# An attention and gated-MLP kernel on one Trainium2 core: the exponentials' output in natural token order instead of chunk order

## The chip, the core and the metric

The kernel runs on one core of a Trainium2 chip. The metric is the device time of one execution, in microseconds (us). Engines are named as in the profile: PE (TensorE matmul), PEld (its weight loads), DVE (VectorE), ACT (ScalarE), POOL (GpSimd), SP (SyncE, which here only issues transfers).

## The reference

For 8 batches, 12 heads, 448 tokens and a head width of 64:

```
q_n, k_n = rmsnorm(q, g_q), rmsnorm(k, g_k)
attn     = softmax(q_n @ k_n.T / 8)
x        = (attn @ v), heads side by side          # [8, 448, 768]
h        = relu(x @ w_in);  u, v = halves of h     # [8, 448, 512] each
v_n      = (v - mean(v)) / sqrt(var(v) + 1e-6)
v_s      = w_spatial @ v_n + b_spatial             # mixes the 448 tokens
out      = (u * v_s) @ w_out                       # [8, 448, 768] float32
```

## The kernel before

Work comes in 24 groups of four heads (three groups to a batch). A load (`op_L`) puts the queries or the keys of a group into a tile `raw` of 128 partitions: 64 partitions for each of two heads, times two heads in the free dimension (`r`). Partition p holds the seven token rows 7p to 7p+6 of its head one after the other, so token t is at (p, c) with t = 7p + c. The c are called chunks here: a chunk is 64 tokens, each seven apart from the next.

For a group the steps are: squares and their sums (`op_Q`, `op_R`), the inverse root (`op_I`, `op_J`), the multiplication `nrm<-raw,rs` (`op_N`), a transposition through SP's queue into `qT` and `kr` (`op_T`, line 493), and a copy of the keys with the gains (`op_Z`). After the transposition the tokens lie along the free dimension in chunk order: first the 64 tokens of chunk 0, then those of chunk 1, and so on (position 64c + p).

`op_S` (line 518) computes the scores of one key chunk for the four heads into two PSUM banks, the 64 keys of two heads along the partitions and the 448 queries along the free dimension. `op_E` (line 526) is one ACT instruction that takes the exponential of both banks, 128 partitions by 896 elements, and writes them in bfloat16 to a tile `et`. There are 7 of these for each group, 168 in all. The sums and the products with v (`op_s`, `op_a`, `op_b`, line 551) run over `et` with the queries as the moving dimension; `op_D` and `op_d` make the reciprocal of the sum (a logarithm and an exponential on ACT), and `op_X` (line 580) multiplies it in and writes `xt`, whose columns are the tokens.

From `xt` on, a batch is one set of matrix products: `op_V` and `op_W` (lines 596 and 625) give v for tiles of 128 tokens, `op_c`, `op_B`, `op_M`, `op_m`, `op_A` normalise it, `op_U` (line 662) gives u, `op_H` (line 676) multiplies with the spatial weights, `op_G` gates, `op_O` (line 690) multiplies with `w_out`, `op_o` evicts to a tile `os` of 128 rows by 768, and `op_t` (lines 711 and 714) stores it.

Since nothing reorders the tokens on the way, all of that is in chunk order as well. An output tile m holds chunk 2m in partitions 0 to 63 and chunk 2m+1 in partitions 64 to 127; in the result, the rows of a chunk are seven apart. So `op_t` stores a full tile with two transfers of 64 rows each, and the last tile (64 rows, chunk 6) with one or two more. The spatial weights have to be in chunk order too. They are loaded in the setup as `w_sp` (line 337; its space is the tile `gt` in the profile's names), transposed by PE in `op_Y` (line 360), whose weight operand picks columns seven apart, and copied to `w_spT` by `op_y` as they come; the bias is read with a step of seven elements and written densely by `op_wx` (both through the helper at lines 373 and 375).

The order of the instructions is written out: `PLAN` is one list of words, such as `E.0.1/0/a` (operation E, group 0, chunk unit 1, slot 0, engine ACT), and every engine's queue takes its own operations in that order. PSUM banks and tile slots are given in the words. The scores of a unit come a few words ahead of its exponential, in banks that an earlier exponential has read. `t` words, squares, reciprocals, evictions and exponentials are interleaved in it; SP issues loads, transpositions and stores in one queue. `port` puts waits between DVE and POOL instructions that use tiles in SBUF, in the order of the list.

Of the kernel before, what the change touches and what calls it, by code (L numbers as in the profile page):

```python
# [11 lines left out]
AF = mybir.ActivationFunctionType  # L12
# [150 lines left out]
def kernel(  # L163
# [14 lines left out]
    B, H, S, D = q.shape  # L178
# [3 lines left out]
    C = 7  # L182
    T = 64
    TAIL = 384
    scale = 1.0 / math.sqrt(D)
    pe, act, dve, pool, sync = nc.tensor, nc.scalar, nc.vector, nc.gpsimd, nc.sync
    engines = {"a": act, "v": dve, "g": pool, "s": sync}
# [4 lines left out]
    ps = psp.tile([128, 8, 512], FP, name="ps")  # L192

    def several(name, n, shape, dt):
        return [const.tile(shape, dt, name=f"{name}{i}") for i in range(n)]
# [7 lines left out]
    ets = several("et", SLOTS["et"], [128, 2, S], BF)  # L203
# [15 lines left out]
    oss = several("os", SLOTS["os"], [128, DM], FP)  # L219
# [7 lines left out]
    w_sp = gt_all.rearrange("p n f s -> p (n f) s")[0:64, 0:C]  # L227
    w_spT = const.tile([128, 4, S], BF, name="w_spT")
# [117 lines left out]

    def op_wx(sl, e):
        assert where["wb"]
        copy(engines[e], w_spT[64:65, 3, :].rearrange("q (c p) -> q c p", p=T),
             oss[-1][64:65, 0:S].rearrange("q (p c) -> q c p", c=C))  # L350
        where["wx"] = True

    def op_Y(sl, e, m):

        n = 1 if m == 3 else 2
        where["Y", m] = sl[0]
        p_ = ps[:, sl[0], :].bitcast(BF)
        for a in range(n):
            for c in range(C):
                pe.matmul(out=p_[64 * a:64 * a + 64, T * c:T * c + T],  # L360
                          lhsT=w_sp[:, c, :].rearrange("q (p c) -> q c p", c=C)[:, 2 * m + a, :],
                          rhs=ident[0:64, 0:64], is_transpose=True, start=(c == 0), stop=(c == C - 1),
                          tile_position=(0, 64 * a))

    def op_y(sl, e, m):
        n = 1 if m == 3 else 2
        p_ = ps[:, where.pop(("Y", m)), :].bitcast(BF)[0:64 * n, 0:S]
        copy(engines[e], w_spT[0:64 * n, m, :], p_)
        where["wT", m] = True

    def copy(eng, out, in_):
        if eng is act:
            act.activation(out=out, in_=in_, func=AF.Copy, bias=0.0, scale=1.0)  # L373
        else:
            eng.tensor_copy(out=out, in_=in_)  # L375
# [147 lines left out]
    def op_E(sl, e, G, u):  # L523
        a, b = where.pop(("S", G, u))
        where["et", G, u] = sl[0]
        act.activation(out=ets[sl[0]], in_=ps[:, a:b + 1:b - a, 0:S], func=AF.Exp, bias=0.0, scale=1.0)  # L526

    def et_of(G, r, c):
        if G or c == 6:
# [69 lines left out]
    def tail_at(b, h):  # L599

        return 0 if b == B - 1 and h == 0 else 64
# [97 lines left out]
             ps[rows, where.pop(("O", b, m, h))[0], 0:384])  # L699
        where["o", b, m, h] = True  # L700

    out_c = [out[b].rearrange("(p c) m -> c p m", c=C) for b in range(B)]

    def op_t(sl, e, b, m):
        t = oss[where["os", b, m]]
        assert where["o", b, m, 0] and where["o", b, m, 1]
        if m == 3:
            for n, at in enumerate(sorted({tail_at(b, 0), tail_at(b, 1)})):
                cols = [h for h in range(2) if tail_at(b, h) == at]
                cols = slice(384 * cols[0], 384 * cols[-1] + 384)  # L710
                engines[(e or "ss")[n]].dma_start(out=out_c[b][6][:, cols], in_=t[at:at + 64, cols])
            return
        for par in range(2):
            engines[(e or "ss")[par]].dma_start(out=out_c[b][2 * m + par], in_=t[64 * par:64 * par + 64])

    def op_z(sl, e, n):
        dummies(sl[0], n)
# [5 lines left out]
    for word in PLAN.split():  # L723
        name, sl, e = (word.split("/") + ["", ""])[:3]
# [32 lines left out]
```

## Time and profile before

| | |
|---|---|
| three runs | 275.09, 276.58 and 278.78 us, median 276.58 |
| the profiled execution | 275.98 us; span from first to last instruction 274.2 us |
| busy: PE, ACT, DVE, POOL | 257.9, 217.8, 203.8, 145.0 us |
| mean granted TensorE clock | 0.985 |

Busy time is the sum of the time in which an engine had an instruction under way. Matmuls are pipelined and their ends are modelled, so PE's busy time is an upper figure. Neighbouring instructions of one engine overlap a little, so a mean duration times a count is somewhat more than the busy time of a group. "Idle before" of a group is time in which its engine stood still just ahead of it, with the instruction that ended the wait.

### The profile page before, as it was taken

To read this page: it belongs to the slowest core of one execution; us is meant where nothing else is said; L and a number is where in the kernel's file an instruction comes from. 1 tells how busy PE (TensorE), PEld (TensorE's weight loads), DVE (VectorE), ACT (ScalarE), POOL (GpSimd) and SP (SyncE) were. 2 spreads that over 40 slices of the span, in tenths; PEclk is the share of its full clock that TensorE was granted. 3 is DMA by queue.
4 is the path that set the end of the run, shared out by engine and by line. 5 is a ranking of instruction groups with operands and counts; after the bars stand their busy time and mean duration, and the time that the engine had idled before them with its cause. 6 is when DMAs were issued, how large, how long until landed. Compare 5 with 4: busy or idle time off the path is not lost.

```text
span 274.2 us, 10148 instructions
## 1 busy us (share of the span) xinstructions
PE 257.9 (94%) x4372; PEld 137.5 (50%) x4389; DVE 203.8 (74%) x355; ACT 217.8 (79%) x357; POOL 145.0 (53%) x122
## 2 busy tenths in 40 slices
PE   7788999999899999999999999989999999999992
PEld 7565564465345455344454454444454545455550
DVE  3788899879859998987985698946976284748730
ACT  4489899999889999988998999988899965330632
POOL 3092994698745898957875669649950000000000
PEclk9959999999999999999999999999999999999998
DMA  7999998999969999999799999976986400114586
GB/s 208 319 344 273 260 171 119 295 204 245 167 145 168 376 177 187 198 251 184 232 184 267 286 246 241 175 95 61 194 114 141 117 2 2 31 29 115 154 279 204
DMA packets 63072, 51.14 MB, mean 187 GB/s; under 512 B 39601, under 2 KB 58674, under 8 KB 63026
## 3 DMA queue, kind: packets, MB, share of 16 engines
q1 hardware_dynamic: 54770, 42.22, 65.4%
q0 software_dynamic: 8256, 8.27, 19.3%
q8 instruction: 34, 0.56, 0.8%
q14 instruction: 12, 0.10, 0.1%
HBM read 38.55 MB, written 11.01 MB: 181 GB/s over the span
## 4 chain that ended last, share of the span: by engine, by line
PE 42%; POOL 13%; DMA 12%; DVE 10%; ACT 10%; issue 10%; SPq 1%; ACTq 0%; POOLq 0%; DVEq 0%
PE ps L551 8%; PE ps L690 7%; POOL nrm L438 7%; PE ps L662 7%; DMA vt<-in_v_dram 6%; ACT et L526 6%; PE ps L676 6%; PE ps L596 5%; PE ps L518 5%; POOL sqt L394 5%; DMA raw<-in_q_dram 3%; DVE ss L405 3%; DMA kr<-nrm 3%; PE ps L625 3%; POOL vt L326 2%
## 5 line engine op out<-in xcount | busy, mean ns | idle before, releaser
L526 ACT ACTIVATE et<-ps 128x896 bf16<-128x896 f32 x168 | 146.1, 923 | 13.4 <-PE ps L518 11.4
L438 POOL TENSOR_TENSOR nrm<-raw,rs 128x896 bf16<-128x896 f32 x40 | 67.3, 1691 | 29.0 <-ACT rs L423 9.4
L518 PE MATMUL ps<-qT,kT 64*32 64x448 bf16 x1344 | 61.1, 357 | 3.2 <-DVE kT L476 1.1
L551 PE MATMUL ps<-et,vt 64*32 64x448 bf16 x1344 | 52.1, 350 | 2.5 <-DMA vt<-in_v_dram 1.0
L394 POOL TENSOR_TENSOR sqt<-raw 128x896 f32<-128x896 f32 x28 | 46.8, 1683 | 13.8 <-DVE vn L653 9.3
L405 DVE TENSOR_REDUCE ss<-sqt 128x14 f32<-128x896 f32 x46 | 48.5, 1076 | 2.9 <-ACT sqt L392 1.2
L662 PE MATMUL ps<-xt,w_in 128*128 128x448 bf16 x192 | 43.4, 353 | 0.2
L518 PEld LDWEIGHTS <-kT 64*32 64x32 bf16 x1344 | 22.2, 90 | 31.7 <-issue 22.5
L690 PE MATMUL ps<-w_out,gt 128*128 128x384 bf16 x192 | 36.5, 326 | 0.1
L580 DVE TENSOR_TENSOR xt<-ps,rc 128x448 bf16<-128x448 f32 x48 | 27.9, 618 | 11.5 <-ACT rc L574 6.9
L596 PE MATMUL ps<-w_in,xt 128*128 128x512 bf16 x127 | 33.9, 380 | 0.9 <-issue 0.3
L551 PEld LDWEIGHTS <-vt 64*32 64x32 bf16 x1344 | 24.9, 92 | 16.2 <-issue 4.2
L373 ACT ACTIVATE os<-ps 128x384 f32<-128x384 f32 (+1 forms) x34 | 16.3, 491 | 15.2 <-PE ps L690 14.6
L551 PE MATMUL ps<-et,ones 64*32 64x448 bf16 x672 | 27.8, 349 | 0.0
L676 PE MATMUL ps<-w_spT,vn 128*128 128x448 bf16 (+1 forms) x128 | 27.7, 353 | 0.2 <-DVE xt L580 0.2
L662 PEld LDWEIGHTS <-w_in 128*128 128x128 bf16 x192 | 17.2, 97 | 20.8 <-issue 7.4
L690 PEld LDWEIGHTS <-gt 128*128 128x128 bf16 x192 | 18.1, 98 | 15.6 <-issue 2.7
L681 DVE TENSOR_TENSOR gt<-ps,us 128x448 bf16<-128x448 f32 x32 | 19.2, 619 | 9.0 <-PE ps L676 5.9
L637 DVE BATCH_NORM_STATS2 s<-vs 128x6 f32<-128x512 bf16 (+1 forms) x32 | 21.9, 683 | 1.6 <-ACT vs L587 1.1
L375 DVE COPY os<-ps 128x384 f32<-128x384 f32 (+1 forms) x30 | 16.5, 555 | 8.9 <-PE ps L690 5.5
L326 POOL DMA_DIRECT2D vt<-in_v_dram x34 | 23.0, 681 | 0.0
L589 DVE TENSOR_SCALAR vs<-ps 128x512 bf16<-128x512 f32 (+1 forms) x24 | 16.3, 683 | 7.4 <-PE ps L596 3.5
(63 smaller groups left out, 253.5 us busy)
## 6 DMA issues: line engine op xcount, KB each, us to landing
out_dram<-os SPq DMA_DIRECT2D x55, 192.0 KB, 3.2
raw<-in_k_dram SPq DMA_DIRECT2D x23, 448.0 KB, 5.9
raw<-in_q_dram SPq DMA_DIRECT2D x23, 448.0 KB, 7.0
vt<-in_v_dram POOLq DMA_DIRECT2D x14, 224.0 KB, 7.3
vt<-in_v_dram POOLq DMA_DIRECT2D x20, 112.0 KB, 5.4
w_in<-in_moe_w_in_dram POOLq DMA_DIRECT2D x8, 192.0 KB, 12.8
w_out<-in_moe_w_out_dram POOLq DMA_DIRECT2D x1, 768.0 KB, 8.2
raw<-in_k_dram SPq DMA_DIRECT2D x2, 224.0 KB, 3.7
```

The source lines that it names most:

```text
L326: pool.dma_start(out=vts[b % 2][64 * halves[0]:64 * halves[0] + 64 * len(halves), g].rearrange("p r c d -> p r (c d)"), in_=src)
L394: port(eng, eng.tensor_tensor(out=t, in0=x, in1=x, op=ALU.mult))
L405: dve.tensor_reduce(out=sss[G % 3][:, i].rearrange("p r c -> p (r c)"), in_=sqt[where.pop(("sq", G, i))].rearrange("p r (c d) -> p (r c) d ...
L438: port(eng, eng.tensor_tensor(out=nrm[sl[0]].rearrange("p c r d -> p r c d"), in0=raw[where["raw", G, i]].rearrange("p r (c d) -> p r c d" ...
L518: pe.matmul(out=ps[at:at + 32, sl[n], 0:S], lhsT=kT[64 * r:64 * r + 64, c, 64 * hh + 32 * x:64 * hh + 32 * x + 32], rhs=qT[64 * r:64 * r + ...
L526: act.activation(out=ets[sl[0]], in_=ps[:, a:b + 1:b - a, 0:S], func=AF.Exp, bias=0.0, scale=1.0)
L551: pe.matmul(out=ps[32 * l:32 * l + 32, where[kind, G][0], 0:S], lhsT=w, rhs=et_of(G, r, c)[at:at + 64], start=(n == 1), stop=(n == C), til ...
L580: dve.tensor_tensor(out=xts[b % 2][:, 2 * g + half, :], in0=ps[:, where.pop(("ab"[half], G))[0], 0:S], in1=rcs[where["rc", G]], op=ALU.mult)
L596: pe.matmul(out=ps[:, bank, :], lhsT=xts[b % 2][:, j, 128 * m:128 * m + 128], rhs=w_in[:, j % 2, j // 2, DH:], start=(n == 1 and j == 2 * ...
L662: pe.matmul(out=ps[:, bank, 0:S], lhsT=w_in[:, j % 2, j // 2, 128 * f:128 * f + 128], rhs=xts[b % 2][:, j, :], start=(n == 1 and j == 2 * ...
L676: pe.matmul(out=ps[:, sl[0], 0:S], lhsT=vns[b % SLOTS["vn"]][rows, m, 128 * f:128 * f + 128], rhs=w_spT[rows, m, :], start=(m == 0), stop= ...
L690: pe.matmul(out=ps[:, sl[0], 0:384], lhsT=gts[b % 2][:, f, 128 * m:128 * m + 128], rhs=w_out[:, f, 384 * h:384 * h + 384], start=(f == 0), ...
```

## The change

The exponential writes its result through a permuted view. It still reads the two PSUM banks in chunk order, one element after the other, and puts the element of (c, p) at position 7p + c: two elements that follow each other in the stream land 7 bfloat16 elements apart. From there on the tokens are in natural order. An output tile m holds rows 128m to 128m+127 and is stored with one transfer; the last tile holds rows 384 to 447. The spatial weights are read densely by `op_Y` and written with a step of seven by `op_y`; the bias is copied densely. `PLAN`, slots and the order of all instructions stay as they are; of each pair of stores of a full tile one is left.

```diff
     def op_wx(sl, e):
-        copy(engines[e], w_spT[64:65, 3, :].rearrange("q (c p) -> q c p", p=T),
-             oss[-1][64:65, 0:S].rearrange("q (p c) -> q c p", c=C))
+        copy(engines[e], w_spT[64:65, 3, :], oss[-1][64:65, 0:S])
...
     def op_Y(sl, e, m):
-                          lhsT=w_sp[:, c, :].rearrange("q (p c) -> q c p", c=C)[:, 2 * m + a, :],
+                          lhsT=w_sp[:, c, 128 * m + 64 * a:128 * m + 64 * a + 64],
...
     def op_y(sl, e, m):
-        copy(engines[e], w_spT[0:64 * n, m, :], p_)
+        copy(engines[e], w_spT[0:64 * n, m, :].rearrange("q (p c) -> q c p", c=C),
+             p_.rearrange("q (c p) -> q c p", c=C))
...
     def op_E(sl, e, G, u):
-        act.activation(out=ets[sl[0]], in_=ps[:, a:b + 1:b - a, 0:S], func=AF.Exp, bias=0.0, scale=1.0)
+        act.activation(out=ets[sl[0]].rearrange("q r (p c) -> q r c p", c=C),
+                       in_=ps[:, a:b + 1:b - a, 0:S].rearrange("q r (c p) -> q r c p", c=C),
+                       func=AF.Exp, bias=0.0, scale=1.0)
...
-    out_c = [out[b].rearrange("(p c) m -> c p m", c=C) for b in range(B)]
-
     def op_t(sl, e, b, m):
...
-                engines[(e or "ss")[n]].dma_start(out=out_c[b][6][:, cols], in_=t[at:at + 64, cols])
+                engines[(e or "ss")[n]].dma_start(out=out[b][TAIL:S, cols], in_=t[at:at + 64, cols])
             return
-        for par in range(2):
-            engines[(e or "ss")[par]].dma_start(out=out_c[b][2 * m + par], in_=t[64 * par:64 * par + 64])
+        engines[(e or "s")[0]].dma_start(out=out[b][128 * m:128 * m + 128], in_=t)
```

## The prediction

> **What bounds the kernel now.** I read the page first, then busy time by stretch, then the chain of waits, then the groups of instructions by shape.
>
> ```profile
> span 274.2 us, 10148 instructions
> PE 257.9 (94%) x4372; PEld 137.5 (50%) x4389; DVE 203.8 (74%) x355; ACT 217.8 (79%) x357; POOL 145.0 (53%) x122
> ACT  4489899999889999988998999988899965330632
> ...
> PE 42%; POOL 13%; DMA 12%; DVE 10%; ACT 10%; issue 10%; SPq 1%; ACTq 0%; POOLq 0%; DVEq 0%
> ```
>
> Over the whole span PE is the busiest engine and leads the chain that ended last. ACT's 79% is an average over two stages: its row of slices stands at 8 or 9 up to slice 32 and falls off after. All exponentials start between 14.4 and 228.9 us (first row below), so I cut the span there (second and third row; columns after the stretch: its length, then busy us and instructions of PE, PEld, DVE, ACT, POOL; granted clock, DMA share, GB/s):
>
> ```profile
> L526 ACT ACTIVATE et<-ps x168: 896/917/982, 14.4 to 228.9; 128x896 bf16<-128x896 f32 x168
> ...
> 14.40:230.00 215.60, 208.83 (x3847) 107.64 (x3869) 172.00 (x287) 196.91 (x312) 141.30 (x112) 0.99 0.94 193
> 230.00:274.20 44.20, 38.76 (x354) 20.63 (x340) 23.32 (x48) 14.17 (x32) 0.00 (x0) 0.98 0.44 126
> ```
>
> In the first stretch ACT works 196.9 of 215.6 us. It has 18.7 us of slack, 9%. Time added to ACT there beyond that slack lengthens the kernel, whatever the chain shows today. In the last 44 us ACT has slack in plenty, and no exponential runs.
>
> ```profile
> L526 ACT ACTIVATE et<-ps 128x896 bf16<-128x896 f32 x168 | 146.1, 923 | 13.4 <-PE ps L518 11.4 <-PE ps L551 1.1
> L373 ACT ACTIVATE os<-ps 128x384 f32<-128x384 f32 x27 | 13.1, 493 | 14.8 <-PE ps L690 14.6
> ...
> ACT et L526 <- PE ps L518: 11.4, 29, 1.1
> ```
>
> The exponentials are 146.1 of ACT's 196.9 us. ACT stood still before them for 13.4 us, of which 11.4 us are 29 waits for scores, none over 1.1 us. The two rows also give ACT's price for each element when it writes densely: (923 - 493) / (896 - 384) = 0.84 ns, on 170 ns that don't depend on the width.
>
> **The exponential's write.** The count of exponentials, their input and their width stay; only the place of each written element moves, to 14 bytes from the one before. No instruction of the trace writes single elements apart, so the price has to be bounded from both sides. A permutation as such is free where the runs are long:
>
> ```profile
> L438 DVE TENSOR_TENSOR nrm<-raw,rs 128x896 bf16<-128x896 f32 x6 | 6.4, 1088 | 1.5 <-POOL nrm L438 1.1 <-POOL nrm L446 0.4
> L394 DVE TENSOR_TENSOR sqt<-raw 128x896 f32<-128x896 f32 x5 | 5.3, 1086 | 1.3 <-POOL nrm L438 0.7 <-POOL sqt L394 0.6
> ```
>
> Line 438 writes a permuted tile in runs of 64 elements and takes 1088 ns, the dense line 394 takes 1086. So the lower end is no price at all: 923 ns as before. Single elements apart are read at two places in the setup:
>
> ```profile
> L360 PEld LDWEIGHTS <-gt 64*64 64x64 bf16 x49 | 4.2, 193 | 2.7 <-issue 1.9 <-DMA gt<-in_moe_w_spatial_dram 0.8
> L551 PEld LDWEIGHTS <-vt 64*32 64x32 bf16 x1344 | 24.9, 92 | 16.2 <-issue 4.2 <-DMA vt<-in_v_dram 1.9
> L625 PEld LDWEIGHTS <-gt 128*64 128x64 bf16 x64 | 6.0, 109 | 1.5 <-issue 0.3
> ...
> L375 DVE CAST w_spT<-os 1x448 bf16<-1x448 f32 x1 | 1.0, 971 | 0.0
> L411 DVE TENSOR_REDUCE ss<-sqt 128x7 f32<-128x448 f32 x4 | 2.4, 618 | 1.9 <-ACT sqt L392 1.9
> L405 DVE TENSOR_REDUCE ss<-sqt 128x14 f32<-128x896 f32 x46 | 48.5, 1076 | 2.9 <-ACT sqt L392 1.2 <-POOL sqt L394 1.2
> ```
>
> Line 360 loads 64 columns that are 7 bfloat16 elements apart, the very step of the new write. It takes 193 ns, where 32 dense columns take 92 and 64 dense ones 109. Dense columns add (109 - 92) / 32 = 0.53 ns each, which leaves 75 ns fixed; the stepped ones come to (193 - 75) / 64 = 1.84 ns each, or, with all of the 92 ns as fixed, 1.58. The bias copy on DVE reads 448 float32 elements 28 bytes apart in 971 ns; dense reads on that engine cost (1076 - 618) / 448 = 1.02 ns each on 161 fixed, so the stepped read costs (971 - 161) / 448 = 1.81 ns. Two engines with different dense prices arrive at 1.6 to 1.8 ns for an element that stands alone. That looks like a price of the memory access, so I expect a write to pay it too: upper end 1.84 ns, lower end of a paid price 1.58. Between "free" and "paid" I take "paid", because the nearest row, line 360, has the same step and the same type; within 1.58 to 1.84 I take 1.68, twice ACT's own 0.84 (an element on every second step, an estimate). One exponential then takes 170 + 896 x 1.68 = 1675 ns, 0.753 us more, and 168 of them add 126.4 us (111 at 1.58, 150 at 1.84).
>
> [...]
>
> **What absorbs it.** The longer exponential gives PE 0.75 us more for each next set of scores. The 29 waits average 0.39 us, so I let all 11.4 us vanish; the ends are nothing and the whole slack of 18.7. No other engine hides more: ACT then has 196.9 + 126.4 = 323.3 us of work in that stretch, PE 208.8, DVE 172.0, POOL 141.3, and what waits behind the exponentials in ACT's queue (the roots for POOL's `nrm`, the reciprocals for DVE's `xt`, evictions) comes later by as much. PE's products read `et` densely before and after, which costs nothing new.
>
> **The stores.** 24 of the 48 transfers of line 714 go.
>
> ```profile
> L714 SPq DMA_DIRECT2D out_dram<-os x48: 466/590/1426, 125.6 to 269.5; - x48
> ...
> SPq L493 <- POOL nrm L438: 68.3, 22, 14.4
> ...
> 255.63 14.45 SPq L714 DMA_DIRECT2D out_dram<-os  x20
> 270.18 1.18 SPq L711 DMA_DIRECT2D out_dram<-os  x2
> ...
> 268.14 0.49 ACT L373 ACTIVATE os<-ps 128x384 f32<-128x384 f32 x1 [0.47 <-PE ps L690]
> 268.90 0.99 ACT L373 ACTIVATE os<-ps 64x384 f32<-64x384 f32 x2 [0.28 <-PE ps L625]
> ```
>
> At 0.590 us each that frees 14.2 us of SP's queue, but SP waits far longer for others (68.3 us for `nrm` alone), so inside the span it is worth nothing; were SP never waiting, it would be at most those 14.2 us. At the end the last eviction is done at 268.90 + 0.99 = 269.89 and the last two stores start at 270.18, since the store ahead holds the queue until 270.08. One issue less lets them start at 269.89: 0.3 us gained. Against it, one transfer of 384 KB may land later than two of 192:
>
> ```profile
> out_dram<-os SPq DMA_DIRECT2D x55, 192.0 KB, 3.2
> raw<-in_k_dram SPq DMA_DIRECT2D x23, 448.0 KB, 5.9
> ```
>
> The last full tile is evicted at 268.14 + 0.49 = 268.63; with the 5.9 us of the larger loads it lands at 274.5, 0.3 us past today's end. I take -0.3, ends -0.3 and +0.3.
>
> **The setup.** The 49 weight loads of line 360 become dense, 193 to 109 ns: 4.1 us of loads; 21 of them stand on the chain with their matmuls (second row below: start and length in us), 21 x 84 ns = 1.8 us at most. The bias copy falls from 971 to about 161 + 448 x 1.02 = 618 ns. Against this the four copies to `w_spT` write single elements:
>
> ```profile
> L360 PE MATMUL ps<-ident,gt 64*64 64x64 bf16 x49 | 4.4, 274 | 1.3 <-DVE w_spT L375 0.9 <-DMA gt<-in_moe_w_spatial_dram 0.4
> 14.12 1.90 PE ps L360 x21
> ...
> L676 PE MATMUL ps<-w_spT,vn x128: 349/353/363, 63.5 to 262.5; 128*128 128x448 bf16 x96, 65*128 65x448 bf16 x32
> L375 DVE COPY w_spT<-ps x2: 381/387/393, 13.7 to 21.4; 128x448 bf16<-128x448 bf16 x2
> L373 ACT ACTIVATE w_spT<-ps x2: 524/530/536, 15.2 to 16.4; 64x448 bf16<-64x448 bf16 x1, 128x448 bf16<-128x448 bf16 x1
> ```
>
> At 1.84 ns the DVE copies take up to 161 + 824 = 985 ns each (+1.2 us in all), and ACT's two 170 + 753 = 923 (+0.8). Line 676 reads `w_spT` only from 63.5 us on; PE waited for such a copy once (0.9 us). These nearly cancel: I take 0, ends -1.8 and +2.
>
> **Sum.** 274.2 + 126.4 - 11.4 - 0.3 = 388.9 us of span. The profiled execution took 275.98, 1.8 more than its span and 0.6 below the median of the runs; with that I predict 391 us. Ends of this case: 274.2 + 111 - 18.7 - 2.1 + 1.8 = 366, and 274.2 + 150 + 2.3 + 1.8 = 428.
>
> **The rivals.**
> *The write is free* (13%). ACT's output side takes single elements at 0.84 ns, the exponential stays at 923 ns, and the stores decide: -0.3 at the end, 276 us, not slower than before; the point from which this turns is an added price under 11.4 us in all, 0.08 ns an element. For it: the trace shows stepped reads only, and ACT's write may be decoupled from its stream. Against it: line 360. The setup's and the stores' ends make 272 to 278 of it; over 2% faster needs 5.5 us of the 14.2 that SP is spared, which I give 3 of the 13%. [...]
>
> *Half the price* (12%): the write overlaps partly, halfway between the ends, 63 us: 274.2 + 63 - 11.4 + 1.8 = 328. Nothing in the trace speaks for a middle value but that reads and writes may differ.
>
> *TensorE's clock falls and PE becomes the bound as well* (12%).
>
> ```profile
> 10.00:11.00 1.00, 0.47 (x8) 0.12 (x8) 1.00 (x2) 0.00 (x0) 0.00 (x0) 1.00 1.02 293
> 11.00:12.00 1.00, 0.61 (x11) 0.52 (x8) 0.47 (x1) 0.29 (x1) 0.00 (x0) 1.00 1.05 380
> 12.00:13.00 1.00, 1.00 (x19) 0.74 (x17) 0.31 (x1) 0.97 (x3) 0.00 (x0) 1.00 1.06 384
> 13.00:14.00 1.00, 0.22 (x8) 0.17 (x1) 1.00 (x2) 0.29 (x2) 0.82 (x1) 0.59 1.06 382
> 14.00:15.00 1.00, 0.88 (x10) 0.87 (x9) 0.60 (x2) 0.94 (x3) 1.00 (x3) 0.50 1.05 376
> ...
> 19.00:20.00 1.00, 1.00 (x24) 0.23 (x24) 1.00 (x2) 0.44 (x1) 1.00 (x3) 0.50 1.19 270
> ```
>
> After 4 us at 57% busy the granted clock was 0.50 for some 6 us. Behind a slow ACT, PE is 208.8 / 330 = 63% busy. At half clock its work for one exponential doubles, 2 x 208.8 / 168 = 2.49 us against ACT's 323.3 / 168 = 1.92; if half of the exponentials fall in such times, 84 x 0.57 = 48 us are added: 439. Against it: gaps will be short and spread, and a slower PE is a busier one.
>
> *More than two steps an element* (6%): three, 2.52 ns, add 253 us and give about 517.
>
> **How the numbers follow.** The main case has 57%. Leaving out the free write (13%) and the three steps (6%), the range goes from just under half the price, 325, to just over the clock's rival, 445. Slower by over 2%, which is about what a measurement here can tell from no change (the runs spread over 1.3%), holds in all cases but the free write: 87%. Within 2%: 10%. Faster: 3%.
>
> **What would show it.** Right: the group of line 526 at about 1675 ns with the same 896 elements, ACT over 95% busy from 14 us to about 45 us before the end, its 11.4 us of waits for scores nearly gone, PE around 60% there, the last stage still some 44 us. The price is a step's if the mean is near 1675 or 2430 and not between. Wrong: line 526 near 923 ns. The clock's rival: PEclk at 0.5 to 0.8 in the middle slices. The stores: 24 issues of 384 KB, and the gap between last eviction and last store closed.

## The result: 2.59 times slower

The changed kernel takes 713.14 us (median of 6 runs, 712.32 to 713.56), the kernel before 275.83 us in the same session. The ratio is 2.588, with a 95% interval of 2.579 to 2.597. The direction was forecast, the size was not: 391 us were predicted, with 445 as the upper end. Here and below, medians are over all runs of a kernel; the ratios leave out disturbed ones, so the two can differ by a few tenths of a per cent.

The page of the changed kernel, busy time, slices of ACT and of the granted clock, and the chain that ended last:

```profile
span 710.5 us, 10114 instructions
PE 407.7 (57%) x4372; PEld 168.9 (24%) x4389; DVE 209.9 (30%) x355; ACT 660.8 (93%) x357; POOL 145.2 (20%) x122
ACT  5999999999999999999999999999999999989623
PEclk8555556655757755675676795585587575576799
...
ACT 75%; issue 13%; PE 9%; DMA 1%; DVE 1%; SPq 0%; ACTq 0%; DVEq 0%
```

The page cuts the span into 40 slices; from the 2nd to the 37th ACT is now busy for 80% or more, and after the last exponential some 45 us are left, as before. One stretch of 100 us (columns as in the prediction), the groups by shape and the waits:

```profile
100.00:200.00 100.00, 55.36 (x568) 19.71 (x565) 27.39 (x45) 99.73 (x49) 22.81 (x16) 0.62 0.28 64
...
L526 ACT ACTIVATE et<-ps 128x896 bf16<-128x896 f32 x168 | 594.4, 3838 | 5.2 <-PE ps L518 4.8
L375 DVE COPY w_spT<-ps 128x448 bf16<-128x448 bf16 x2 | 3.8, 1876 | 0.0
...
POOL nrm L438 <- ACT rs L423: 233.9, 17, 33.5
PE ps L518 <- ACT et L526: 173.8, 91, 3.2
...
ACT et L526 <- PE ps L518: 4.8, 7, 1.5
```

One exponential went from 923 to 3838 ns. The group's busy time rose from 146.1 to 594.4 us, by 448.3 us. That is the whole loss: ACT's busy time rose by 660.8 - 217.8 = 443.0 us, its idle time fell from 56.4 to 49.7, and the span rose by 436.3. (168 times 3838 ns would be 645 us: neighbouring exponentials overlap, and one takes 594.4 / 168 = 3.54 us of ACT's time.) Everyone waits for ACT now (PE for banks and `et`, POOL for the roots), and ACT waits for scores 4.8 us in all.

### The profile page after: what moved, and what is told of

It is laid out like the page before. It is cut to its first block, busy times and chain, and to the rows that moved or that the text cites. A ratio compares the mean times of both kernels' runs of the same rounds, so it can differ in the third digit from the quotient of the medians.

```text
span 710.5 us, 10114 instructions
## 1 busy us (share of the span) xinstructions
PE 407.7 (57%) x4372; PEld 168.9 (24%) x4389; DVE 209.9 (30%) x355; ACT 660.8 (93%) x357; POOL 145.2 (20%) x122
## 4 chain that ended last, share of the span: by engine, by line
ACT 75%; issue 13%; PE 9%; DMA 1%; DVE 1%; SPq 0%; ACTq 0%; DVEq 0%
ACT et L526 69%; PE ps L692 2%; PE ps L553 2%; PE ps L664 1%; ACT sqt L392 1%; DMA raw<-in_q_dram 1%; PE ps L678 1%; ACT rc L576 1%; PE ps L518 1%; ACT rc L572 1%; ACT os L373 1%; PE ps L598 1%; DVE ss L405 1%; ACT rs L423 1%; ACT w_spT L373 0%
## 5 line engine op out<-in xcount | busy, mean ns | idle before, releaser
L526 ACT ACTIVATE et<-ps 128x896 bf16<-128x896 f32 x168 | 594.4, 3838 | 5.2 <-PE ps L518 4.8
L518 PE MATMUL ps<-qT,kT 64*32 64x448 bf16 x1344 | 98.3, 485 | 204.6 <-ACT et L526 173.8
L553 PE MATMUL ps<-et,vt 64*32 64x448 bf16 x1344 | 81.1, 473 | 12.4 <-ACT et L526 8.7
L664 PE MATMUL ps<-xt,w_in 128*128 128x448 bf16 x192 | 62.9, 472 | 14.1 <-ACT et L526 11.3
L553 PE MATMUL ps<-et,ones 64*32 64x448 bf16 x672 | 50.2, 558 | 15.2 <-ACT et L526 7.8
L692 PE MATMUL ps<-w_out,gt 128*128 128x384 bf16 x192 | 47.8, 395 | 9.3 <-ACT et L526 7.3
L598 PE MATMUL ps<-w_in,xt 128*128 128x512 bf16 x127 | 46.6, 491 | 6.8 <-ACT et L526 3.4
L678 PE MATMUL ps<-w_spT,vn 128*128 128x448 bf16 (+1 forms) x128 | 41.0, 473 | 9.5 <-ACT et L526 9.3
L591 DVE TENSOR_SCALAR us<-ps 128x448 bf16<-128x448 f32 x22 | 13.5, 621 | 50.5 <-PE ps L664 50.3
L553 PEld LDWEIGHTS <-ones 64*32 64x32 bf16 x672 | 18.2, 129 | 33.4 <-issue 32.9
```

The source lines that it names most:

```text
L518: pe.matmul(out=ps[at:at + 32, sl[n], 0:S], lhsT=kT[64 * r:64 * r + 64, c, 64 * hh + 32 * x:64 * hh + 32 * x + 32], rhs=qT[64 * r:64 * r + ...
L526: act.activation(out=ets[sl[0]].rearrange("q r (p c) -> q r c p", c=C), in_=ps[:, a:b + 1:b - a, 0:S].rearrange("q r (c p) -> q r c p", c= ...
L553: pe.matmul(out=ps[32 * l:32 * l + 32, where[kind, G][0], 0:S], lhsT=w, rhs=et_of(G, r, c)[at:at + 64], start=(n == 1), stop=(n == C), til ...
L591: dve.tensor_relu(out=out, in_=in_)
L598: pe.matmul(out=ps[:, bank, :], lhsT=xts[b % 2][:, j, 128 * m:128 * m + 128], rhs=w_in[:, j % 2, j // 2, DH:], start=(n == 1 and j == 2 * ...
L664: pe.matmul(out=ps[:, bank, 0:S], lhsT=w_in[:, j % 2, j // 2, 128 * f:128 * f + 128], rhs=xts[b % 2][:, j, :], start=(n == 1 and j == 2 * ...
```

## The experiments

### Writes and reads by themselves

A kernel with five instructions of each kind, one after the other on their engine, from PSUM or from a tile in SBUF. Beside them run only stores of a constant and, at the start, fills of the input tiles by POOL. ACT's and DVE's writes were not under way together; ACT's reads, though, ran beside DVE's first writes. In short:

```
a_perm:  out = t.rearrange("q r (p c) -> q r c p"), in = two banks, as in the change
a_exp / d_copy(type, step, run): out = tile viewed as (p, step)[:, :, 0:run], in = PSUM, dense
a_read:  out dense, in = two banks read 64 elements apart
reads:   out dense bfloat16, in = tile in SBUF, one element of every 7
```

> Nothing of the reference is computed; ACT and DVE instructions stand alone, five of each kind, and write bfloat16 or float32 elements out of PSUM densely, 2, 4, 7 or 8 elements apart, and in runs of two or four with gaps between the runs; some read single elements and write densely. In the changed kernel the exponential took 3838 ns, (3838 - 170) / 896 = 4.1 ns for each element. Theory A (a price of small pieces): every written piece below some width costs about 4 ns by itself, on ACT and DVE alike; then the permuted exponential takes about 3.7 us here too, with steps of 2, 4, 7 and 8 alike, runs of two or four bfloat16 elements cost a half, a quarter or less for each element, and float32 elements 7 apart are cheap, 1.7 ns or less. Theory B (a price of hops): any hop costs 4 ns, so float32 elements 7 apart cost as much as bfloat16 ones, and small steps (2, 4) cost less than 7. Theory C (contention in the full kernel): alone, the permuted exponential takes 1.0 to 1.7 us, and the rest came from the other engines. Reads of single elements, the row of the prediction: A and B expect 1.6 to 1.9 ns an element on DVE for float32 7 apart if the bias copy told the truth, 1.0 if it had only waited for POOL. The exponential that reads PSUM 64 elements apart and writes densely: 923 ns if such reads are free, 1.7 us or more if not.

The groups by shape; `ab` and `af` are ACT's bfloat16 and float32 writes, `vb` and `vf` DVE's, `arb`, `arf`, `vrf` reads:

```profile
L48 ACT ACTIVATE ab_dense<-ps 128x896 bf16<-128x896 f32 x5 | 4.6, 917 | 1.9 <-DVE ps L32 1.8
L52 ACT ACTIVATE ab_perm<-ps 128x896 bf16<-128x896 f32 x5 | 18.2, 3631 | 0.1
L57 ACT ACTIVATE ab_readperm<-ps 128x896 bf16<-128x896 f32 x5 | 4.8, 970 | 0.1
L48 ACT ACTIVATE ab_two<-ps 128x896 bf16<-128x896 f32 x5 | 5.8, 1161 | 0.1
L48 ACT ACTIVATE ab_four<-ps 128x896 bf16<-128x896 f32 x5 | 10.7, 2147 | 0.1
L48 ACT ACTIVATE ab_seven<-ps 128x896 bf16<-128x896 f32 x5 | 18.3, 3652 | 0.1
L48 ACT ACTIVATE ab_eight<-ps 128x896 bf16<-128x896 f32 x5 | 20.9, 4182 | 0.1
L48 ACT ACTIVATE ab_run_two<-ps 128x896 bf16<-128x896 f32 x5 | 5.2, 1030 | 0.1
L48 ACT ACTIVATE af_two<-ps 128x448 f32<-128x448 f32 x5 | 2.8, 562 | 0.1
L48 ACT ACTIVATE af_seven<-ps 128x448 f32<-128x448 f32 x5 | 4.8, 962 | 0.1
L79 DVE CAST vb_seven<-ps 128x448 bf16<-128x448 f32 x5 | 9.5, 1903 | 0.1
L79 DVE COPY vf_seven<-ps 128x448 f32<-128x448 f32 x5 | 4.7, 949 | 0.1
L97 ACT ACTIVATE arb_dense<-sarb_dense 128x448 bf16<-128x448 bf16 x5 | 2.9, 574 | 0.1
L97 ACT ACTIVATE arb_seven<-sarb_seven 128x448 bf16<-128x448 bf16 x5 | 4.5, 896 | 0.1
L97 ACT ACTIVATE arf_seven<-sarf_seven 128x448 bf16<-128x448 f32 x5 | 5.0, 1009 | 0.1
L99 DVE CAST vrf_dense<-svrf_dense 128x448 bf16<-128x448 f32 x5 | 2.0, 392 | 0.1
L99 DVE CAST vrf_seven<-svrf_seven 128x448 bf16<-128x448 f32 x5 | 2.8, 565 | 0.1
```

The permuted exponential alone takes 3631 ns, so theory C falls: the 0.2 us more that the mean in the full kernel shows is within what neighbours overlap there. Less the prediction's 170 ns, the bfloat16 steps 2, 4, 7 and 8 cost 1.11, 2.21, 3.89 and 4.48 ns an element. That grows with the step, which theory A did not expect. Float32 at step 7 costs 1.77 ns on ACT, so theory B, which expected 4, falls too. A's main point stands: pairs of bfloat16, 28 bytes apart, are written in 1030 ns. DVE pays the same as ACT, (1903 - 161) / 448 = 3.89 and (949 - 161) / 448 = 1.76 ns with the prediction's 161 ns, so the price of a write does not come from ACT's own stepping; that it is the memory's is the author's reading and was not shown.

Reads differ from that. A read of single bfloat16 elements from SBUF costs ACT (896 - 200) / 448 = 1.55 ns (200 being what 574 leaves beside 448 elements at the dense 0.84), one of float32 elements 28 bytes apart (1009 - 200) / 448 = 1.81. DVE reads the latter in (565 - 161) / 448 = 0.90 ns, about the 1.0 that was expected if the bias copy had told of something else than its read. So these two engines don't share a price of reads, with the reserve that ACT's reads were not alone. Reading PSUM 64 elements apart costs almost nothing: 970 against 917 ns.

### One rule for the writes

The figures of that run can be fitted with lines of 16 bytes, an estimate from them and nothing that a trace shows by itself: 4.48 ns for each line that gets lone halves of a 4-byte word (step 2: a quarter of a line for each element, 1.12; step 4: 2.24; step 7: 3.92), 1.77 ns for each line that gets whole words. This was put to the test with other steps, 448 elements each, with the first run's helpers and these calls, in short (POOL's products ran beside ACT's first groups, the rest one after the other):

```
for a_exp on ACT and d_copy on DVE:
    BF16: dense, steps 3, 5, 7, 16; pairs every 14 from element 1; pairs every 4; fours every 28 from element 1
    FP32: steps 3, 4, 8
POOL: products written as BF16 dense, BF16 step 7, FP32 step 7
```

> Nothing of the reference is computed; instructions of 448 elements stand alone, five of each kind. The first such run fits one rule on both engines: the time goes by 16-byte lines, about 1.77 ns for each line that whole 4-byte words are written to and about 4.5 ns for each line that gets lone 2-byte halves, or the engine's own dense time where that is longer. Rule L expects beyond the dense fixed part, for ACT and DVE alike: bfloat16 steps 3, 5, 7 and 16 at 1.7, 2.8, 3.9 and 4.5 ns an element (16 no dearer than 8 was); pairs on an odd element, which cover two halves of two words, at the price of lone halves, 4.5 ns a pair or more (1.2 us and more an instruction more than the even pairs); pairs with a gap of one pair free; float32 steps 3, 4 and 8 at 1.3, 1.8 and 1.8 ns. Rival P (the price grows with the step, no lines): step 16 at 9 ns, float32 step 8 at twice step 4. Rival H (the price is per lone piece, whatever its alignment): odd pairs as even ones, about 1.0 ns an element. POOL is open: its dense product of 448 should take about 0.9 us; by the same memory price at least 448 x 3.9 = 1.7 us with the step of 7.

```profile
L45 ACT ACTIVATE ab_three<-ps 128x448 bf16<-128x448 f32 x5 | 4.6, 916 | 0.1
L45 ACT ACTIVATE ab_five<-ps 128x448 bf16<-128x448 f32 x5 | 7.1, 1417 | 0.1
L45 ACT ACTIVATE ab_sixteen<-ps 128x448 bf16<-128x448 f32 x5 | 10.5, 2092 | 0.1
L45 ACT ACTIVATE ab_pair_odd<-ps 128x448 bf16<-128x448 f32 x5 | 7.3, 1452 | 0.1
L45 ACT ACTIVATE af_three<-ps 128x448 f32<-128x448 f32 x5 | 3.8, 764 | 0.1
L45 ACT ACTIVATE af_four<-ps 128x448 f32<-128x448 f32 x5 | 4.8, 952 | 0.1
L45 ACT ACTIVATE af_eight<-ps 128x448 f32<-128x448 f32 x5 | 4.9, 977 | 0.1
L51 DVE CAST vb_sixteen<-ps 128x448 bf16<-128x448 f32 x5 | 10.3, 2059 | 0.1
L71 POOL TENSOR_TENSOR gb_seven<-src 128x448 bf16<-128x448 f32 x5 | 9.6, 1928 | 0.3
L71 POOL TENSOR_TENSOR gb_dense<-src 128x448 bf16<-128x448 f32 x5 | 4.7, 932 | 2.1 <-DVE src L30 1.8
```

Steps 3, 5 and 16 cost 1.67, 2.78 and 4.29 ns: step 16 is no dearer than step 8 with its 4.48, so in these runs the price does not grow beyond step 8, 16 bytes (rival P expected 9). Float32 steps 3, 4 and 8 cost 1.33, 1.75 and 1.80. Pairs on an odd element take (1452 - 170) / 224 = 5.7 ns a pair where even pairs took (1030 - 170) / 448 = 1.9, so rival H falls: at the same 28 bytes between the pairs it was the lone half words that were dear, not the short piece. (The price of a pair came out as rule L had it, 4.5 or more; the difference for an instruction, 224 x 3.8 ns = 0.85 us, did not reach the 1.2 us that were expected beside it.) DVE follows ACT (step 16: (2059 - 161) / 448 = 4.24 ns), and POOL's product at step 7 takes 1928 ns, twice its dense one and at most 1928 / 448 = 4.3 ns an element. Why a line of half words costs 2.5 times a line of whole words (4.48 against 1.77 ns by the fit) was not tried and stays open.

### The exponential's write set back

```diff
-        act.activation(out=ets[sl[0]].rearrange("q r (p c) -> q r c p", c=C),
-                       in_=ps[:, a:b + 1:b - a, 0:S].rearrange("q r (c p) -> q r c p", c=C),
-                       func=AF.Exp, bias=0.0, scale=1.0)
+        act.activation(out=ets[sl[0]], in_=ps[:, a:b + 1:b - a, 0:S], func=AF.Exp, bias=0.0, scale=1.0)
```

> The changed kernel with the exponential's write alone set back to dense; stores, spatial weights and bias stay as changed, so tokens in chunk order meet weights and stores in natural order. If the exponential's write is the whole loss: line 526 back at 923 ns, 274 to 277 us, ratio to the kernel before 0.995 to 1.005, with up to 0.3 us gained by the single stores at the end. If stores, setup or the clock carry a part of the loss: above 281 us (over 2%).

Tokens in chunk order then meet weights and stores in natural order, so this kernel leaves the right order out and computes something else than the reference, with instructions of the same number and shapes. 280.12 us, ratio 1.0121 (1.0082 to 1.0159), the exponential at 927 ns. Of the 437 us, 433 go with this one edit. What is left, 1.2%, is more than the first theory's 0.5% and less than the rival's 2%, so neither had it right. Its place shows in the tile `w_spT` and in the stretches of the start (columns as in the prediction):

```profile
L526 ACT ACTIVATE et<-ps 128x896 bf16<-128x896 f32 x168 | 146.6, 927 | 13.5 <-PE ps L518 12.3 <-PE ps L551 0.3
...
L375 DVE COPY w_spT<-ps x2: 1880/1886/1892, 14.7 to 24.4; 128x448 bf16<-128x448 bf16 x2
L373 ACT ACTIVATE w_spT<-ps x2: 1900/1907/1914, 17.2 to 19.8; 64x448 bf16<-64x448 bf16 x1, 128x448 bf16<-128x448 bf16 x1
...
PE ps L359: 3.9, 1
...
22.00:26.00 4.00, 2.26 (x32) 1.42 (x30) 3.56 (x3) 4.00 (x8) 1.13 (x2) 0.50 1.15 282
26.00:30.00 4.00, 3.51 (x48) 1.36 (x51) 3.91 (x6) 2.48 (x3) 0.56 (x1) 0.50 1.13 260
30.00:34.00 4.00, 4.00 (x58) 2.45 (x54) 2.46 (x4) 2.48 (x4) 3.02 (x2) 0.65 1.09 242
```

The four setup copies write single halves too and take 1.9 us each in place of 0.4 to 0.5. PE waits for one of them 3.9 us (0.9 before), and its granted clock stays at half until about 33 us (20 before).

### The permutation moved to the read

The same permutation with dense writes; the input is read 64 elements apart:

```diff
-        act.activation(out=ets[sl[0]].rearrange("q r (p c) -> q r c p", c=C),
-                       in_=ps[:, a:b + 1:b - a, 0:S].rearrange("q r (c p) -> q r c p", c=C),
+        act.activation(out=ets[sl[0]].rearrange("q r (p c) -> q r p c", c=C),
+                       in_=ps[:, a:b + 1:b - a, 0:S].rearrange("q r (c p) -> q r p c", c=C),
```

> The full computation with the whole change, but the exponential does its permutation on the side of the read: it takes the elements of PSUM 64 apart and writes 896 dense bfloat16 elements. If PSUM reads of single elements are free: exponential near 923 ns, 274 to 278 us. If a read of a single element costs 1.6 to 1.8 ns, as the prediction read from the two setup rows: exponential 1.6 to 1.8 us, 370 to 430 us. If reads cost as much as writes did: about 710 us.

279.87 us, ratio 1.0116 (1.0040 to 1.0192); the exponential takes 928 ns, as dense:

```profile
L526 ACT ACTIVATE et<-ps 128x896 bf16<-128x896 f32 x168 | 146.6, 928 | 12.5 <-PE ps L518 10.7 <-PE ps L553 1.0
```

In this kernel that order of reading PSUM is free for the exponential, and the whole change is there without its price, but for the 1.2% that the run before had left too.

The other place for it, later and rarer (24 logarithms and 48 multiplications to `xt`, exponentials dense in chunk order):

```diff
-        act.activation(out=rcs[sl[0]], in_=ps[:, where.pop(("s", G))[0], 0:S], func=AF.Ln, bias=0.0, scale=1.0)
+        act.activation(out=rcs[sl[0]].rearrange("q (p c) -> q p c", c=C),
+                       in_=ps[:, where.pop(("s", G))[0], 0:S].rearrange("q (c p) -> q p c", c=C),
+                       func=AF.Ln, bias=0.0, scale=1.0)
...
-        dve.tensor_tensor(out=xts[b % 2][:, 2 * g + half, :], in0=ps[:, where.pop(("ab"[half], G))[0], 0:S],
-                          in1=rcs[where["rc", G]], op=ALU.mult)
+        dve.tensor_tensor(out=xts[b % 2][:, 2 * g + half, :].rearrange("q (p c) -> q p c", c=C),
+                          in0=ps[:, where.pop(("ab"[half], G))[0], 0:S].rearrange("q (c p) -> q p c", c=C),
+                          in1=rcs[where["rc", G]].rearrange("q (p c) -> q p c", c=C), op=ALU.mult)
```

> The full computation, natural order from xt on, exponentials dense: the permutation is done by the 24 logarithms of the sums (ACT) and the 48 multiplications to xt (DVE), which read PSUM 64 elements apart and write densely. If such reads are free: 274 to 277 us, ratio 0.99 to 1.00, and this would be the change without its price. If a read costs 1.7 ns an element: DVE's multiplication goes from 618 to about 920 ns, 48 x 0.3 = 14 us on DVE, which is busy 172 of 215.6 us, and ACT's logarithm from 551 to 930 ns, 24 x 0.38 = 9 us within 18.7 us of slack: 276 to 290 us. If a read costs 4 ns: 48 x 1.3 = 64 us on DVE, 300 us or more.

280.43 us, ratio 1.0136 (1.0080 to 1.0192): the same again. DVE's multiplication stays at 617 ns (618 before). For free reads 274 to 277 us had been expected here and 274 to 278 in the run above; both missed, by what the next run puts down to the setup copies that they still had.

### The setup's copies too

Exponentials with permuted reads, and:

```diff
-        copy(engines[e], w_spT[0:64 * n, m, :].rearrange("q (p c) -> q c p", c=C),
-             p_.rearrange("q (c p) -> q c p", c=C))
+        copy(engines[e], w_spT[0:64 * n, m, :].rearrange("q (p c) -> q p c", c=C),
+             p_.rearrange("q (c p) -> q p c", c=C))
```

> The full computation with natural order; the exponentials and the four copies to the spatial weights both read PSUM in permuted order and write densely. If the 1.2% that the run with permuted reads of the exponentials alone was over the kernel before came from the stepped writes of those four copies (1.9 us each in place of 0.4 to 0.5, with TensorE's clock at half until 28 us): 274 to 276.5 us, ratio 0.993 to 1.002, clock back at full by 22 us. If it came from the permuted reads of 168 exponentials or from the larger stores: 279 to 280 us again.

277.09 us, ratio 1.0003 (0.9963 to 1.0042): level with the kernel before. The copies take 620 and 532 ns, and the clock is back by 23 us. (For DVE the permuted read is not free here: dense, its bfloat16 copy took 387 ns. These are two copies.)

```profile
L375 DVE COPY w_spT<-ps x2: 615/620/625, 14.2 to 21.5; 128x448 bf16<-128x448 bf16 x2
...
22.00:26.00 4.00, 3.75 (x82) 1.99 (x81) 3.91 (x6) 4.00 (x7) 1.12 (x2) 0.92 1.15 281
```

So the setup's share of the loss was the stepped writes of four small copies; whether it went by PE's wait or by the longer time at half clock was not separated. The expected bound for the clock, full by 22 us, was missed by about a microsecond.

### The single store undone

On top of the last kernel:

```diff
-        engines[(e or "s")[0]].dma_start(out=out[b][128 * m:128 * m + 128], in_=t)
+        for par in range(2):
+            engines[(e or "ss")[par]].dma_start(out=out[b][128 * m + 64 * par:128 * m + 64 * par + 64],
+                                                in_=t[64 * par:64 * par + 64])
```

> As the run before this one (permuted reads, dense writes, natural order), but every full output tile is stored by two transfers of 64 rows again, so the single store is undone by itself. By the prediction's working the single store is worth 0.3 us at the end: this one 0 to 0.6 us slower. If the larger transfer lands later or holds the queue: this one up to 1 us faster. If SP's queue mattered inside the span: 2 us or more slower.

276.66 us, ratio 1.0029 (0.9993 to 1.0065). Its interval overlaps that of the single store; one transfer or two makes no difference that these runs can tell. The traces do show the end that the prediction worked out. SP's queue and the last evictions, first with the single store, then with two:

```profile
257.29 13.36 SPq L713 DMA_DIRECT2D out_dram<-os  x10
271.08 1.12 SPq L711 DMA_DIRECT2D out_dram<-os  x2
...
270.57 0.99 ACT L373 ACTIVATE os<-ps 64x384 f32<-64x384 f32 x2 [0.28 <-PE ps L627]
```

```profile
256.10 14.44 SPq L714 DMA_DIRECT2D out_dram<-os  x20
270.63 1.19 SPq L711 DMA_DIRECT2D out_dram<-os  x2
...
269.37 0.99 ACT L373 ACTIVATE os<-ps 64x384 f32<-64x384 f32 x2 [0.28 <-PE ps L627]
```

With one store the last two begin while the last eviction is still running (271.08 against 271.56), with two 0.27 us after it (270.63 against 270.36). From the end of the last eviction to the end of the span it is 3.8 us with one and 4.3 with two, in one trace each.

## Why the prediction was wrong

**The bound, right.** ACT's slack in the first stretch was the right place to look: it was 91% busy there and is 99.7 of 100 us busy from 100 to 200 us now; the chain of waits, which named PE, would have hidden it.

**The price, wrong.** The step that failed is "I expect a write to pay it too". The rows under it were reads, and the write has another price. A write of whole words 28 bytes apart costs about what they showed, 1.77 ns. But the change writes half words, and 14 bytes apart these cost 3.89 ns an element. With 3.9 in place of 1.68 the exponential is 170 + 896 x 3.9 = 3664 ns, and the prediction's own sum gives 274.2 + 168 x 2.741 - 11.4 - 0.3 = 723 us of span, where 710.5 were measured; so this one term is nearly the whole miss. (Most of the other 12.5 us is overlap of neighbours: the group's busy time rose by 448.3 us and not by 168 x 2.741 = 460.5.) The prediction's upper rival, 2.52 ns, had only 6%, and the upper bound of 1.84 was no bound: it came from rows that showed reads alone. "On every second step" was a guess about ACT's own stepping; the equal price on DVE, 3.89 ns at step 7 on both, shows that ACT doesn't set it.

**Both rows misread.** Line 360's 193 ns were taken as the time of one load. The row says more: 49 loads keep PEld busy for 4.2 us, 86 ns each, so they overlap, and a duration divided by 64 columns is not a price of a column. That its 1.58 lies beside the 1.55 of ACT's bfloat16 reads was luck. The bias copy's 971 ns was taken as its own time. Alone, on 128 partitions, the stepped copy takes 565 ns and the dense one 392, while in the changed kernel the dense one took 1506 (timeline of that kernel):

```profile
88.40 3.48 POOL L438 TENSOR_TENSOR nrm<-raw,rs 128x896 bf16<-128x896 f32 x2 [12.07 <-ACT rs L423]
88.83 1.51 DVE L375 CAST w_spT<-os 1x448 bf16<-1x448 f32 x1
```

POOL's line 438 ran beside it, and did so before the change too (from 38.4 to 41.8 us, the copy from 40.6). The dense copy probably waited for POOL: with the setup's permuted reads it ends at 43.28 us, 0.26 after the instruction of line 438 that it started beside (41.34 + 1.68 = 43.02), and with the exponential's dense write at 47.27, 0.25 after its one (43.68 + 3.34 = 47.02). The stepped copy of the kernel before did not wait so long: it ended at 41.59, ahead of POOL's 41.77. What stretched it from 565 to 971 ns was not tried by itself and stays open. So the second witness for "1.6 to 1.8 ns" was no witness either, and that the two agreed was chance.

**What absorbs it, right in kind.** 11.4 us were let vanish; ACT's idle time fell by 6.7. Waits for scores went from 11.4 to 4.8 us, not to nothing.

**The setup, wrong in size.** Zero was taken with an end of +2; it cost 1.2%, 3.8 us (280.12 us with the exponential's write set back, against 276.29). The copies were mis-sized by the same price, 1.9 us each in place of 0.92 to 0.99 (ACT's 923 ns was besides worked out with 1.68 ns, where the sentence says 1.84), and the wait of PE for such a copy was costed without the clock, which stayed at half for some 13 us longer. The 4.1 us of spared loads could not be either: all 49 had kept PEld busy for 4.2 us, and dense they still take 2.1 to 2.2.

**The stores, right.** The single store starts the last stores earlier, and no run can tell it in the time. In the two kernels that differ by the stores alone, the larger transfers landed no later than the small ones, so the fear of a later landing was not borne out (median from issue to landing, last column):

```profile
out_dram<-os SPq DMA_DIRECT2D x24, 384.0 KB, 2.9
...
out_dram<-os SPq DMA_DIRECT2D x55, 192.0 KB, 3.2
```

**The rivals.** The clock did fall, to 0.663 on average, and cost next to nothing: PE's busy time grew to 407.7 us, but ACT waited only 4.8 us for its scores. The free write is out. Its time would have come out had the permutation been on the read of PSUM, with the exponential at 928 ns and, with the setup's copies changed too, 277.09 us.

## What to carry to other kernels

Put a permutation on the side that reads PSUM and write SBUF densely: the exponential's reads 64 elements apart cost 928 against 927 ns here, the same permutation on the write 3838. Check the copies all the same: DVE's bfloat16 copy went from 387 to 620 ns. If a write has to hop, keep its pieces to whole aligned 4-byte words: here ACT wrote 896 bfloat16 elements in 1030 ns as even pairs 28 bytes apart, in 3652 as single ones 14 bytes apart. And a bound on an unseen operation is only as good as the nearest row's kind: a row that shows a read bounds no write, and a row of 4-byte pieces none of 2 bytes.

## What was not expected of the hardware

- Single bfloat16 elements written to SBUF at steps 7, 8 and 16 cost ACT 3.89, 4.48 and 4.29 ns an element, at steps 7 and 16 DVE 3.89 and 4.24, and at step 7 POOL at most 4.3; float32 elements at steps 4, 7 and 8 cost ACT 1.75, 1.77 and 1.80. By the fit above that is about 4.5 and 1.77 ns for each line of 16 bytes, an estimate from these figures. Pairs of bfloat16 28 bytes apart took ACT 5.7 ns a pair from an odd element on, 1.9 from an even one.
- ACT's exponential read PSUM 64 float32 elements apart in 970 ns for 896 elements, densely in 917.
- In the changed kernel an ACT instruction behind a slow write started before that write had ended: a logarithm starts at 87.39 us, the exponential ahead of it ends at 84.18 + 3.65 = 87.83. So means grow without more work (the logarithms of the sums: mean 632 ns, 551 before; median 546, 544 before).
